# Loads of q, k and v over 128 partitions instead of two halves of 64, and attention matmuls as quarter-array tiles

## The chip, the cores and the metric

The kernel runs on one core of a Trainium2 chip. The metric is device time in microseconds (us), the median of several executions. A ratio is the mean time of one kernel's fast runs over the mean of the other's fast runs of the same rounds on the same chip, with a 95% interval, so it is not quite the ratio of the medians that stand beside it. A profiled execution gives a span, from its first to its last instruction; the run's time is about 2 us longer.

## The reference, cut to what matters

```python
# q, k, v: [8 batches, 8 heads, 576, 64], float32
q_s = softmax(q, over the 64)            # within a row
k_s = softmax(k, over the 576)           # along the sequence
kv  = einsum('bhsd,bhse->bhde', k_s, v)  # 64 x 64 for each head
x   = einsum('bhsd,bhde->bhse', q_s, kv) # then [8, 576, 512], heads side by side
xn  = layer_norm(x) * g_ln
out = x + relu(xn @ w_ch1) @ w_ch2       # 512 -> 2048 -> 512
```

The MLP is most of the work; it runs over nine chunks of 512 tokens (one for each batch, the last for the 64 tokens that each batch has left over). Attention needs 28 MB of q, k and v, in 48 half loads of 590 KB (one tensor, one batch, four of the eight heads).

## The kernel before

The program is written as a list of tasks. A small scheduler puts them in order when the program is built, so that each engine's instructions stand in the program in a fixed order. The scheduler takes the loads' queue to move 0.34 MB per us:

```python
if mb or land:
    queue = max(queue, end) + mb / 0.34
    end = queue + land
```

A half load is two DMAs, each into 64 partitions. Heads 0 to 3 lie on the lower half, heads 4 to 7 on the upper (`R` = `D` = 64, `JT` = 9):

```python
for e in range(2):
    load(stg[s][R * e : R * e + R].rearrange("p (h r) -> p h r", h=2),
         src[b].rearrange("(e h) (p j) d -> e p h (j d)", e=2, j=JT)[e, :, 2 * hf : 2 * hf + 2],
         [("stg", s, e)], 128, 0.295)
```

The queue's DMAs stand in program order too. From batch 2 on, the loads of v stand behind a DMA transpose of exp(q) of the same batch, through `gate`:

```python
lq = [load_half(b, q, hf) for hf in range(2)]
lk = [load_half(b, k, hf) for hf in range(2)]
# ... exp(q), its row sums; for b >= 2:
    state["eqT"] = (plan.add("SP", 0.7, lambda: nc.sync.dma_start_transpose(eqT[u], ...)),)
    gate[0] = state["eqT"]            # loads from here on follow this transpose
lv = [load_half(b, v, hf) for hf in range(2)]
```

TensorE (PE) multiplies exp(k) by v (the kv matmuls) for two heads of one half at a time (weights 64x128, 130 columns), so that half of the result is of no use; VectorE (DVE) scales it and multiplies by a mask, which leaves a block-diagonal weight. That multiplies the transposed exp(q) with the whole array:

```python
for j in range(JT):
    for e in range(2):
        nc.tensor.matmul(pa[ab[e]][:, :130], ek[u][r0 : r0 + R, hf, j, :], vb[u][r0 : r0 + R, hf, j]..., ...)
# DVE: kve[u][:, g, :] = pa * rz * mask
for g in (0, 2, 1, 3):
    nc.tensor.matmul(pa[a], kve[u][:, g, :], et[:, g % 2, 0:8, c0 : c0 + R], ...)
```

ScalarE (ACT) copies the product out as x transposed; a second kind of DMA transpose (`x<-xsT`) brings it back for DVE's batch norm and for the residual. It goes through the same queue as the loads (SPq on the page).

The softmax here doesn't subtract the row's maximum and nothing guards it: scores larger than these inputs give would overflow.

Of the kernel before, what the change touches and what calls it, by code (L numbers as in the profile page):

```python
# [13 lines left out]
FP16 = mybir.dt.float16  # L14
# [119 lines left out]
def dve_t(n, mode=1):  # L134
    return 0.15 + n / (960.0 * mode)
# [3 lines left out]
def kernel(  # L139
# [10 lines left out]
    nc = tc.nc  # L150
# [18 lines left out]
    def sb(shape, dt, name):  # L169
        return persist.tile(shape, dt, name=name, tag=name)  # L170
# [5 lines left out]
    mask = sb([P, P], FP16, "mask")  # L176
# [8 lines left out]
    kve = [sb([P, G, P], FP16, f"kve{i}") for i in range(2)]  # L185
# [27 lines left out]
    def nxt(what, n):  # L213
        i = cnt[what] % n
        cnt[what] += 1
        return i


    def init():
        plan.add("ACT", 1.3, lambda: nc.scalar.add_instruction(mybir.InstLoadActFuncSet(  # L220
            name=nc.get_next_instruction_name(), engine=mybir.EngineType.Activation, act_func_set_id=6)), cls=-1)
        plan.add("DVE", 0.3, lambda: nc.vector.memset(zero.bitcast(U32), 0), w=["zero"])  # L222
        plan.add("DVE", 0.1, lambda: nc.vector.memset(eps, 1e-6 * GS * GS), w=["eps"])
        plan.add("DVE", 0.1, lambda: nc.vector.memset(ones, 1.0 / DM), w=["ones"])
        plan.add("POOL", 1.5, lambda: make_identity(nc, ident), w=["ident"])
        plan.add("POOL", 0.2, lambda: nc.gpsimd.memset(mask.bitcast(U32), 0), w=["mask"])
        for i in range(2):
            plan.add("POOL", 0.1, lambda i=i: nc.gpsimd.memset(mask[64 * i : 64 * i + 64, 64 * i : 64 * i + 64], 1.0), w=["mask"])
        for i in range(2):
            plan.add("POOL", 0.2, lambda i=i: nc.gpsimd.memset(vb[i][:, :, :, :, D], 1.0), w=[("vb", i, h) for h in range(2)])  # L230
        for ko in range(KO1):
            plan.add("ACT", 0.4, lambda ko=ko: nc.scalar.dma_start(
                g_sb[:, ko : ko + 1], moe_g_ln[ko * P : (ko + 1) * P, None]), w=[("g", ko)], land=3.0)
        plan.add("POOL", 0.1, lambda: nc.gpsimd.tensor_scalar_mul(g_sb, in0=g_sb, scalar1=GS),
                 r=[("g", ko) for ko in range(KO1)], w=[("g", ko) for ko in range(KO1)])
# [11 lines left out]
    def load_half(b, src, hf):  # L247

        s = nxt("stg", NST)
        for e in range(2):  # L250
            load(stg[s][R * e : R * e + R].rearrange("p (h r) -> p h r", h=2),
                 src[b].rearrange("(e h) (p j) d -> e p h (j d)", e=2, j=JT)[e, :, 2 * hf : 2 * hf + 2],
                 [("stg", s, e)], 128, 0.295)
        return s
# [24 lines left out]
    def centre_w1(blk):  # L279
# [5 lines left out]
        if blk:  # L285
            plan.add("DVE", dve_t(1024, 2), lambda: nc.vector.tensor_tensor(
                ws, w1_sb[:, 0:2, cs], w1_sb[:, 2:4, cs], op=ALU.add), r=wk, w=["ws"], cls=0)
            src = [ws[:, 0], ws[:, 1]]
        def f():
# [6 lines left out]
            r=["nm"], w=wk, cls=1 if blk == 0 else 0)  # L296
# [16 lines left out]
    def attn(b, early, between=None):  # L313
# [49 lines left out]
        for hf in range(2):  # L363
# [11 lines left out]
            def fm(hf=hf, ab=ab):  # L375
                for j in range(JT):
                    for e in range(2):
                        r0 = R * e
                        nc.tensor.matmul(pa[ab[e]][:, :130], ek[u][r0 : r0 + R, hf, j, :],  # L379
                                         vb[u][r0 : r0 + R, hf, j].rearrange("p s d -> p (s d)"),  # L380
                                         start=(j == 0), stop=(j == JT - 1))
            plan.add("PE", 0.95, fm, r=[("ek", u, hf), ("vb", u, hf)], w=[("pa", a) for a in ab], cls=0)
            for e in range(2):
                a, g = ab[e], 2 * e + hf
                plan.add("DVE", 0.08, lambda a=a, g=g: nc.vector.reciprocal(rz[:, g : g + 1], pa[a][:, D : D + 1]),
                         r=[("pa", a)], w=[("rz", g)], cls=0)
                def fs(a=a, g=g):
                    nc.vector.scalar_tensor_tensor(
                        kve[u][:, g, :].rearrange("p (s d) -> p s d", s=2),
                        in0=pa[a][:, :130].rearrange("p (s c) -> p s c", s=2)[:, :, :D], scalar=rz[:, g : g + 1],  # L390
                        in1=mask.rearrange("p (s d) -> p s d", s=2), op0=ALU.mult, op1=ALU.mult)
                plan.add("DVE", dve_t(128), fs, r=[("pa", a), ("rz", g), "mask"], w=[("kve", u, g)], cls=0)
# [3 lines left out]
        for g in (0, 2, 1, 3):  # L396
            a = nxt("pa", 4)
            c0 = R * (g // 2)
            plan.add("PE", 0.22, lambda g=g, a=a, c0=c0: nc.tensor.matmul(  # L399
                pa[a], kve[u][:, g, :], et[:, g % 2, 0:8, c0 : c0 + R], start=True, stop=True),  # L400
                r=[("eqT", u, g % 2), ("kve", u, g)], w=[("pa", a)], cls=0)
            pv = pa[a].rearrange("p (j t) -> p j t", j=J)
            if early:
                for hf in range(2):
                    js = slice(2 * hf, 2 * hf + 2)
                    w = [("xsT", u, 2 * hf, g), ("xsT", u, 2 * hf + 1, g)]
                    if g // 2 == 0:
                        plan.add("ACT", act_t(256), lambda g=g, js=js, pv=pv: nc.scalar.copy(xt[:, g, js], pv[:, js]), r=[("pa", a)], w=w, cls=0)
                    else:
                        plan.add("DVE", dve_t(256), lambda g=g, js=js, pv=pv: nc.vector.tensor_copy(xt[:, g, js], pv[:, js]), r=[("pa", a)], w=w, cls=0)  # L410
            else:
                plan.add("ACT", act_t(512), lambda g=g, pv=pv: nc.scalar.copy(xt[:, g], pv), r=[("pa", a)],  # L412
                         w=[("xsT", u, j, g) for j in range(J)], cls=0)
        a = nxt("pa", 4)
        def f8(a=a):
            for g in range(G):
                c0 = R * (g // 2)
                nc.tensor.matmul(pa[a][:, R * g : R * g + R], kve[u][:, g, :], et[:, g % 2, 8, c0 : c0 + R], start=True, stop=True)  # L418
        plan.add("PE", 0.3, f8, r=[("eqT", u, 2)] + [("kve", u, g) for g in range(G)], w=[("pa", a)], cls=0)
        c0 = R * (b % 2)  # L420
        plan.add("ACT", act_t(256), lambda a=a: nc.scalar.copy(
            xT8[:, 4 * (b // 2) : 4 * (b // 2) + 4, c0 : c0 + R], pa[a][:, : R * G].rearrange("p (g t) -> p g t", g=G)),
            r=[("pa", a)], w=[("xT8", b)])
# [4 lines left out]
    def tokens(c, cls=1):  # L428

        x, xk, sti, stk = xof(c)  # L430
        if c < B:
            src, r = xsT[c % 2], XK(c % 2)
        else:
            src, r = xT8, [("xT8", b) for b in range(B)]
# [23 lines left out]
    def mm1(c, by_half, split):  # L458

        xt = (xsT[c % 2] if c < B else xT8).rearrange("p (j k) t -> p k j t", j=J)  # L460
        xkeys = XK(c % 2) if c < B else [("xT8", b) for b in range(B)]
# [239 lines left out]
```

## Time and profile before

| | before |
|---|---|
| time, median of 3 executions | 313.81 us (313.08 to 314.52) |
| the profiled execution: its time, its span | 311.52, 309.6 us |
| q, k, v alone in the queue | 230 to 237 GB/s |
| first MLP matmul | 27.07 us |
| first block of 48 wide matmuls of the second chunk | 72.25 us |

The table of waits (engine, what it waited to do, what ended the wait: us in total, times, longest):

```profile
ACT eq L324 <- DMA stg<-in_q_dram: 21.3, 11, 5.2
...
ACT ek L364 <- DMA stg<-in_k_dram: 13.7, 12, 2.5
...
ACT vb L372 <- DMA stg<-in_v_dram: 8.0, 6, 4.1
...
DVE bst L439 <- DMA x<-xsT: 5.4, 4, 2.2
```

Then the page's busy line, and of its DMA issues the transposes of x (last column: median us from issue to landing):

```profile
PE 280.9 (91%) x2017; PEld 173.5 (56%) x2017; DVE 197.4 (64%) x407; ACT 161.8 (52%) x258; POOL 36.6 (12%) x32
```

```profile
x<-xsT SPq DMA_TRANSPOSE x8, 6.4
```

### The profile page before, as it was taken

What the parts mean: (1) busy time and instruction counts of PE and PEld (TensorE: products, weight loads), DVE (VectorE), ACT (ScalarE), POOL (GpSimd) and SP (SyncE); (2) the same over time, 40 slices, a digit from 0 to 9 for tenths busy, and PEclk for the clock granted to TensorE, in tenths of its full rate; (3) what the DMA queues carried; (4) which work ended last, traced back from release to release, by engine and by line L of the source; (5) the groups of instructions that cost most, each with busy time, mean ns of one, the idle gap of its engine ahead of it and who ended that gap; (6) DMA issues with size and microseconds to landing.
All of it is one profiled execution on the core that took longest, in us unless ns stands there. A gap on an engine that the chain in (4) does not pass through costs nothing. (4 is left out here: it accounts for less than half of the span.)

```text
span 309.6 us, 5175 instructions
## 1 busy us (share of the span) xinstructions
PE 280.9 (91%) x2017; PEld 173.5 (56%) x2017; DVE 197.4 (64%) x407; ACT 161.8 (52%) x258; POOL 36.6 (12%) x32
## 2 busy tenths in 40 slices
PE   8749798779999959999898979999999999999992
PEld 3326343445576427845683468447745864784681
DVE  0839999799696516953956499239644973652452
ACT  3625654458774559267556960776388037206500
POOL 2004023005022000050040030201300000000000
PEclk9997999999999979999999999999999999999998
DMA  7999999999996999269989990999993440013004
GB/s 160 267 273 386 280 332 238 236 255 214 228 226 108 196 259 217 54 159 228 233 160 234 286 181 4 210 215 224 160 269 82 83 115 22 2 23 115 0 1 138
DMA packets 56697, 54.74 MB, mean 177 GB/s; under 512 B 35680, under 2 KB 35680, under 8 KB 56672
## 3 DMA queue, kind: packets, MB, share of 16 engines
q1 hardware_dynamic: 56096, 54.41, 75.6%
q8 instruction: 16, 0.26, 0.4%
q10 hardware_dynamic: 576, 0.00, 0.1%
q14 instruction: 9, 0.07, 0.1%
HBM read 36.70 MB, written 9.44 MB: 149 GB/s over the span
## 5 line engine op out<-in xcount | busy, mean ns | idle before, releaser
L450 ACT ACTIVATE hT<-pg 128x512 f16<-128x512 f32 x138 | 80.7, 598 | 61.5 <-PE pg L486 55.3
L486 PE MATMUL pg<-xsT,w_sb 128*128 128x512 f16 x480 | 109.3, 382 | 2.3 <-DVE ot L570 1.2
L486 PEld LDWEIGHTS <-w_sb 128*128 128x128 f16 x544 | 52.7, 98 | 64.8 <-issue 4.4
L502 DVE TENSOR_TENSOR S<-hT 128x1024 f16<-128x1024 f16 x32 | 23.8, 748 | 55.6 <-ACT hT L450 55.6
L562 PEld LDWEIGHTS <-S 128*128 128x128 f16 x512 | 50.0, 98 | 8.0 <-issue 1.4
L562 PE MATMUL pg<-T,S 128*128 128x256 f16 x384 | 43.7, 273 | 1.2 <-DVE cp L570 1.2
L332 POOL TENSOR_TENSOR eq<-eq,rzq 128x1152 bf16<-128x1152 bf16 x12 | 25.8, 2155 | 145.8 <-issue 52.3
L562 PEld LDWEIGHTS <-hT 128*128 128x128 f16 x384 | 37.3, 98 | 7.4 <-issue 1.2
L562 PE MATMUL pg<-w_sb,hT 128*128 128x256 f16 x256 | 30.2, 273 | 0.8 <-ACT hT L450 0.8
L324 ACT ACTIVATE eq<-stg 128x1152 bf16<-128x1152 f32 x16 | 18.6, 1169 | 21.3 <-DMA stg<-in_q_dram 21.3
L439 DVE BATCH_NORM_STATS2 bst<-x 128x6 f32<-128x512 f16 x36 | 24.0, 668 | 5.4 <-DMA x<-xsT 5.4
L327 DVE TENSOR_REDUCE zq<-eq 128x18 f32<-128x1152 bf16 x16 | 21.4, 1340 | 7.3 <-ACT eq L324 7.3
L364 ACT ACTIVATE ek<-stg 128x1152 bf16<-128x1152 f32 x16 | 18.7, 1167 | 13.8 <-DMA stg<-in_k_dram 13.7
L570 DVE SCALAR_TENSOR_TENSOR ot<-pg,st,cp 128x256 f32<-128x256 f32 x48 | 20.9, 477 | 6.9 <-PE pg L562 6.6
L570 DVE SCALAR_TENSOR_TENSOR cp<-pg,st,x 128x256 f32<-128x256 f32 x48 | 20.9, 477 | 4.5 <-PE pg L562 4.3
L379 PE MATMUL pa<-vb,ek 64*128 64x130 f16 x288 | 11.4, 220 | 10.6 <-DVE vb L369 6.6
L372 ACT CAST vb<-stg 128x1152 f16<-128x1152 f32 x12 | 14.0, 1168 | 8.1 <-DMA stg<-in_v_dram 8.0
L379 PEld LDWEIGHTS <-ek 64*128 64x128 bf16 x288 | 9.0, 95 | 15.7 <-issue 12.6
L630 PE MATMUL pg<-zero 128*128 128x512 f16 x51 | 14.8, 447 | 1.2 <-DVE zero L222 1.2
L562 PE MATMUL pg<-T,hT 128*128 128x256 f16 x128 | 15.3, 273 | 0.0
L562 PE MATMUL pg<-w_sb,S 128*128 128x256 f16 x128 | 15.3, 272 | 0.0
L611 PE MATMUL pg<-w_sb,hT 128*128 128x512 f16 x64 | 14.6, 379 | 0.0
(63 smaller groups left out, 215.7 us busy)
## 6 DMA issues: line engine op xcount, KB each, us to landing
stg<-in_q_dram SPq DMA_DIRECT2D x32, 288.0 KB, 7.1
stg<-in_k_dram SPq DMA_DIRECT2D x32, 288.0 KB, 9.6
stg<-in_v_dram SPq DMA_DIRECT2D x32, 288.0 KB, 5.3
out_dram<-ot SPq DMA_DIRECT2D x36, 256.0 KB, 3.7
stg<-in_moe_w_ch_dram SPq DMA_DIRECT2D x16, 512.0 KB, 10.3
x<-xsT SPq DMA_TRANSPOSE x8, 6.4
eqT<-eq SPq DMA_TRANSPOSE x6, 4.6
g_sb<-in_moe_g_ln_dram ACTq DMA_DIRECT2D x4, 0.5 KB, 4.4
```

The source lines that it names most:

```text
L324: plan.add("ACT", act_t(QW), lambda hf=hf, e=e: nc.scalar.activation(e.rearrange("p j (s d) -> p s j d", s=2), sv(lq[hf]), AF.Exp), r=sk(l ...
L327: plan.add("DVE", dve_t(QW), lambda hf=hf, eh=eh: nc.vector.reduce_sum(zq[:, hf], eh, axis=AX.X), r=[("eq", u, hf)], w=[("zq", hf)], cls=cls)
L332: plan.add(eng, dve_t(QW) if early else 2.6, lambda hf=hf, eh=eh, e2=e2: e2.tensor_tensor(eh, eh, rzq[:, hf].to_broadcast([P, 2 * JT, D]), ...
L364: plan.add("ACT", act_t(QW), lambda hf=hf: nc.scalar.activation(ek[u][:, hf].rearrange("p j (s d) -> p s j d", s=2), sv(lk[hf]), AF.Exp), ...
L379: nc.tensor.matmul(pa[ab[e]][:, :130], ek[u][r0 : r0 + R, hf, j, :], vb[u][r0 : r0 + R, hf, j].rearrange("p s d -> p (s d)"), start=(j == ...
L439: plan.add("DVE", dve_t(512), lambda j=j: nc.vector.bn_stats(bst[:, j, :], x[:, j, :]), r=[(xk, j)], w=[("bst", j)], cls=cls)
L450: nc.scalar.activation(hT[:, m, :], pg[gi], AF.Relu)
L486: nc.tensor.matmul(pg[gi], w1_sb[:, ko, m * P : m * P + P], xt[:, ko], start=(ko == 0), stop=(ko == KO1 - 1))
L502: plan.add("DVE", dve_t(256 * n, 2), lambda: nc.vector.tensor_tensor(S[i][:, ks], a, b, op=op), r=r, w=sk(i))
L562: nc.tensor.matmul(pg[gi][:, 256 * i : 256 * i + 256], fa(k, i), fb(k), start=(first and i == 0 and k == 0), stop=(last and k == HK - 1), ...
L570: nc.vector.scalar_tensor_tensor(dst[:, i, :], in0=pg[gi][:, 256 * i : 256 * i + 256], scalar=sti[:, 4, 2 * t0 + i : 2 * t0 + i + 1], in1= ...
L630: nc.tensor.matmul(bank_, zero[:, :P], zero, start=start, stop=start, skip_group_check=True)
```

## The change

The intent is twofold. One DMA for each half load now reaches all 128 partitions, with even heads on the lower half and odd ones on the upper. And the attention matmuls become four concurrent 64x64 tiles, so that no result is thrown away and the mask goes. The core of the diff (cut: buffers, the mask's set-up, the copies of the last 64 tokens, and a few constants of the scheduler):

```diff
-        for e in range(2):
-            load(stg[s][R * e : R * e + R].rearrange("p (h r) -> p h r", h=2),
-                 src[b].rearrange("(e h) (p j) d -> e p h (j d)", e=2, j=JT)[e, :, 2 * hf : 2 * hf + 2],
-                 [("stg", s, e)], 128, 0.295)
+        load(stg[s].rearrange("p (h r) -> p h r", h=2),
+             src[b].rearrange("(h e) (p j) d -> (e p) h (j d)", e=2, j=JT)[:, 2 * hf : 2 * hf + 2],
+             sk(s), 256, 0.59)
...
                     for e in range(2):
-                        r0 = R * e
-                        nc.tensor.matmul(pa[ab[e]][:, :130], ek[u][r0 : r0 + R, hf, j, :],
-                                         vb[u][r0 : r0 + R, hf, j].rearrange("p s d -> p (s d)"), ...)
+                        for i in range(2):
+                            r0, c0 = R * e, D * i
+                            nc.tensor.matmul(pa[ab[e]][c0 : c0 + D, :VW], ek[u][r0 : r0 + R, hf, j, c0 : c0 + D],
+                                             vb[u][r0 : r0 + R, hf, j, i, :], ...)
...
-                    nc.vector.scalar_tensor_tensor(..., in1=mask..., op0=ALU.mult, op1=ALU.mult)
+                nc.vector.tensor_scalar_mul(kve[u][:, g, :], in0=pa[a][:, :D], scalar1=rz[:, g : g + 1])
...
-        for g in (0, 2, 1, 3):
-            nc.tensor.matmul(pa[a], kve[u][:, g, :], et[:, g % 2, 0:8, c0 : c0 + R], ...)
+                for i in range(2):
+                    for e in range(2):
+                        r0, c0 = D * i, R * e
+                        nc.tensor.matmul(pa[ab[i]][c0 : c0 + D, :], kve[u][r0 : r0 + D, 2 * hf + e, :],
+                                         et[r0 : r0 + D, hf, 0:8, c0 : c0 + R], ...)
```

More of the change, by code (lines that the diff above doesn't have):

```diff
@@ L175 @@
     ident = sb([P, P], FP16, "ident")
-    mask = sb([P, P], FP16, "mask")
     zero = sb([P, 512], FP16, "zero")
@@ L184 @@
     eqT = [sb([P, 2 * JT, P], BF16, f"eqT{i}") for i in range(2)]
-    kve = [sb([P, G, P], FP16, f"kve{i}") for i in range(2)]
+    kve = [sb([P, G, D], FP16, f"kve{i}") for i in range(2)]
     xb = [sb([P, J, DM], FP16, f"x{i}") for i in range(3)]
@@ L225, in init @@
         plan.add("POOL", 1.5, lambda: make_identity(nc, ident), w=["ident"])
-        plan.add("POOL", 0.2, lambda: nc.gpsimd.memset(mask.bitcast(U32), 0), w=["mask"])
-        for i in range(2):
-            plan.add("POOL", 0.1, lambda i=i: nc.gpsimd.memset(mask[64 * i : 64 * i + 64, 64 * i : 64 * i + 64], 1.0), w=["mask"])
         for i in range(2):
@@ L232, in init @@
             plan.add("ACT", 0.4, lambda ko=ko: nc.scalar.dma_start(
-                g_sb[:, ko : ko + 1], moe_g_ln[ko * P : (ko + 1) * P, None]), w=[("g", ko)], land=3.0)
-        plan.add("POOL", 0.1, lambda: nc.gpsimd.tensor_scalar_mul(g_sb, in0=g_sb, scalar1=GS),
+                g_sb[:, ko : ko + 1], moe_g_ln[ko * P : (ko + 1) * P, None]), w=[("g", ko)])
+        plan.add("POOL", 4.5, lambda: nc.gpsimd.tensor_scalar_mul(g_sb, in0=g_sb, scalar1=GS),
                  r=[("g", ko) for ko in range(KO1)], w=[("g", ko) for ko in range(KO1)])
@@ L286, in centre_w1 @@
             plan.add("DVE", dve_t(1024, 2), lambda: nc.vector.tensor_tensor(
-                ws, w1_sb[:, 0:2, cs], w1_sb[:, 2:4, cs], op=ALU.add), r=wk, w=["ws"], cls=0)
+                ws, w1_sb[:, 0:2, cs], w1_sb[:, 2:4, cs], op=ALU.add), r=wk, w=["ws"])
             src = [ws[:, 0], ws[:, 1]]
@@ L295, in centre_w1 @@
             w1_sb[:, :, cs], w1_sb[:, :, cs], nm.unsqueeze(1).to_broadcast([P, KO1, 512]), op=ALU.subtract),
-            r=["nm"], w=wk, cls=1 if blk == 0 else 0)
+            r=["nm"], w=wk, cls=0)
     def load_w2(k0, eng="DVE"):
@@ L377, in fm @@
                     for e in range(2):
-                        r0 = R * e
-                        nc.tensor.matmul(pa[ab[e]][:, :130], ek[u][r0 : r0 + R, hf, j, :],
-                                         vb[u][r0 : r0 + R, hf, j].rearrange("p s d -> p (s d)"),
-                                         start=(j == 0), stop=(j == JT - 1))
-            plan.add("PE", 0.95, fm, r=[("ek", u, hf), ("vb", u, hf)], w=[("pa", a) for a in ab], cls=0)
+                        for i in range(2):
+                            r0, c0 = R * e, D * i
+                            nc.tensor.matmul(pa[ab[e]][c0 : c0 + D, :VW], ek[u][r0 : r0 + R, hf, j, c0 : c0 + D],
+                                             vb[u][r0 : r0 + R, hf, j, i, :], start=(j == 0), stop=(j == JT - 1))
@@ L383, in attn @@
+            plan.add("PE", 0.6, fm, r=[("ek", u, hf), ("vb", u, hf)], w=[("pa", a) for a in ab], cls=0)
             for e in range(2):
-                a, g = ab[e], 2 * e + hf
+                a, g = ab[e], 2 * hf + e
                 plan.add("DVE", 0.08, lambda a=a, g=g: nc.vector.reciprocal(rz[:, g : g + 1], pa[a][:, D : D + 1]),
                          r=[("pa", a)], w=[("rz", g)], cls=0)
-                def fs(a=a, g=g):
-                    nc.vector.scalar_tensor_tensor(
-                        kve[u][:, g, :].rearrange("p (s d) -> p s d", s=2),
-                        in0=pa[a][:, :130].rearrange("p (s c) -> p s c", s=2)[:, :, :D], scalar=rz[:, g : g + 1],
-                        in1=mask.rearrange("p (s d) -> p s d", s=2), op0=ALU.mult, op1=ALU.mult)
@@ L392, in attn @@
-                plan.add("DVE", dve_t(128), fs, r=[("pa", a), ("rz", g), "mask"], w=[("kve", u, g)], cls=0)
+                plan.add("DVE", dve_t(64), lambda a=a, g=g: nc.vector.tensor_scalar_mul(
+                    kve[u][:, g, :], in0=pa[a][:, :D], scalar1=rz[:, g : g + 1]),
+                    r=[("pa", a), ("rz", g)], w=[("kve", u, g)], cls=0)
         et = eqT[u].rearrange("p (q j) t -> p q j t", q=2)
         xt = xsT[u].rearrange("p (j k) t -> p k j t", j=J)
-        for g in (0, 2, 1, 3):
-            a = nxt("pa", 4)
-            c0 = R * (g // 2)
-            plan.add("PE", 0.22, lambda g=g, a=a, c0=c0: nc.tensor.matmul(
-                pa[a], kve[u][:, g, :], et[:, g % 2, 0:8, c0 : c0 + R], start=True, stop=True),
-                r=[("eqT", u, g % 2), ("kve", u, g)], w=[("pa", a)], cls=0)
-            pv = pa[a].rearrange("p (j t) -> p j t", j=J)
-            if early:
-                for hf in range(2):
-                    js = slice(2 * hf, 2 * hf + 2)
-                    w = [("xsT", u, 2 * hf, g), ("xsT", u, 2 * hf + 1, g)]
-                    if g // 2 == 0:
-                        plan.add("ACT", act_t(256), lambda g=g, js=js, pv=pv: nc.scalar.copy(xt[:, g, js], pv[:, js]), r=[("pa", a)], w=w, cls=0)
-                    else:
-                        plan.add("DVE", dve_t(256), lambda g=g, js=js, pv=pv: nc.vector.tensor_copy(xt[:, g, js], pv[:, js]), r=[("pa", a)], w=w, cls=0)
-            else:
-                plan.add("ACT", act_t(512), lambda g=g, pv=pv: nc.scalar.copy(xt[:, g], pv), r=[("pa", a)],
-                         w=[("xsT", u, j, g) for j in range(J)], cls=0)
@@ L414, in attn, with fx @@
-        a = nxt("pa", 4)
-        def f8(a=a):
-            for g in range(G):
-                c0 = R * (g // 2)
-                nc.tensor.matmul(pa[a][:, R * g : R * g + R], kve[u][:, g, :], et[:, g % 2, 8, c0 : c0 + R], start=True, stop=True)
-        plan.add("PE", 0.3, f8, r=[("eqT", u, 2)] + [("kve", u, g) for g in range(G)], w=[("pa", a)], cls=0)
-        c0 = R * (b % 2)
-        plan.add("ACT", act_t(256), lambda a=a: nc.scalar.copy(
-            xT8[:, 4 * (b // 2) : 4 * (b // 2) + 4, c0 : c0 + R], pa[a][:, : R * G].rearrange("p (g t) -> p g t", g=G)),
-            r=[("pa", a)], w=[("xT8", b)])
+        for hf in range(2):
+            ab = [nxt("pa", 4) for _ in range(2)]
+            def fx(hf=hf, ab=ab):
+                for i in range(2):
+                    for e in range(2):
+                        r0, c0 = D * i, R * e
+                        nc.tensor.matmul(pa[ab[i]][c0 : c0 + D, :], kve[u][r0 : r0 + D, 2 * hf + e, :],
+                                         et[r0 : r0 + D, hf, 0:8, c0 : c0 + R], start=True, stop=True)
+            plan.add("PE", 0.35, fx, r=[("eqT", u, hf), ("kve", u, 2 * hf), ("kve", u, 2 * hf + 1)], w=[("pa", a) for a in ab], cls=0)
+            for i in range(2):
+                a, g = ab[i], 2 * hf + i
+                pv = pa[a].rearrange("p (j t) -> p j t", j=J)
+                if early:
+                    for th in range(2):
+                        js = slice(2 * th, 2 * th + 2)
+                        w = [("xsT", u, 2 * th, g), ("xsT", u, 2 * th + 1, g)]
+                        if i == 0:
+                            plan.add("ACT", act_t(256), lambda g=g, js=js, pv=pv: nc.scalar.copy(xt[:, g, js], pv[:, js]), r=[("pa", a)], w=w, cls=th / 2)
+                        else:
+                            plan.add("DVE", dve_t(256), lambda g=g, js=js, pv=pv: nc.vector.tensor_copy(xt[:, g, js], pv[:, js]), r=[("pa", a)], w=w, cls=th / 2)
+                else:
+                    plan.add("ACT", act_t(512), lambda g=g, pv=pv: nc.scalar.copy(xt[:, g], pv), r=[("pa", a)],
+                             w=[("xsT", u, j, g) for j in range(J)], cls=0)
@@ new lines, in attn, with f8 @@
+        ab = [nxt("pa", 4) for _ in range(2)]
+        def f8(ab=ab):
+            for hf in range(2):
+                for i in range(2):
+                    for e in range(2):
+                        r0, c0 = D * i, R * e
+                        nc.tensor.matmul(pa[ab[i]][c0 : c0 + D, R * hf : R * hf + R], kve[u][r0 : r0 + D, 2 * hf + e, :],
+                                         et[r0 : r0 + D, hf, 8, c0 : c0 + R], start=True, stop=True)
+        plan.add("PE", 0.2, f8, r=[("eqT", u, 2)] + [("kve", u, g) for g in range(G)], w=[("pa", a) for a in ab], cls=0)
@@ L425, in xof @@
+        c0 = R * (b % 2)
+        for i in range(2):
+            plan.add("ACT", act_t(128), lambda i=i, a=ab[i]: nc.scalar.copy(
+                xT8.rearrange("p (t q s) c -> p t s q c", q=2, s=2)[:, b // 2, i, :, c0 : c0 + R],
+                pa[a][:, : 2 * R].rearrange("p (q t) -> p q t", q=2)),
+                r=[("pa", ab[i])], w=[("xT8", b, i)])
     def xof(c):
@@ L433, in tokens @@
         else:
-            src, r = xT8, [("xT8", b) for b in range(B)]
+            src, r = xT8, [("xT8", b, i) for b in range(B) for i in range(2)]
         i = plan.add("SP", 0.7, lambda: nc.sync.dma_start_transpose(x, src.rearrange("p n t -> p (n t)")) if False else
@@ L460, in mm1 @@
         xt = (xsT[c % 2] if c < B else xT8).rearrange("p (j k) t -> p k j t", j=J)
-        xkeys = XK(c % 2) if c < B else [("xT8", b) for b in range(B)]
+        xkeys = XK(c % 2) if c < B else [("xT8", b, i) for b in range(B) for i in range(2)]
         order = [m + 8 * i for m in range(HK) for i in range(2)] if split else list(range(KO2))
```

## The prediction

> **What bounds the kernel now.** I read the page's busy table first: PE is busy for 280.9 of 309.6 us (91%), DVE for 197.4, ACT for 161.8. Then the chain that ended last: from 225 us to the end it is PE matmuls alone, back to back. So in the later stages a microsecond counts only if it leaves PE's own stream or one of its pauses. Then PE's timeline, for the pauses. Here are the first mm1 matmul, the waits of the second batch's attention, and the longest pause:
>
> ```profile
> 27.07 3.22 PE L473 MATMUL pg<-xsT,w_sb 128*128 128x256 f16 x28
> ...
> 54.56 0.61 PE L341 MATMUL pa<-ident_b,eq 128*128 128x128 bf16 x8 [1.25 <-DVE eq L332]
> ...
> 60.04 0.70 PE L379 MATMUL pa<-vb,ek 64*128 64x130 f16 x18 [1.73 <-DVE vb L369]
> 60.68 1.04 PE L611 MATMUL pg<-w_sb,hT 128*128 128x512 f16 x4
> 62.56 0.70 PE L379 MATMUL pa<-vb,ek 64*128 64x130 f16 x18 [0.85 <-DVE vb L369]
> ...
> 68.08 3.54 PE L473 MATMUL pg<-xsT,w_sb 128*128 128x256 f16 x31 [0.90 <-ACT xsT L408]
> ...
> 111.47 0.72 PE L379 MATMUL pa<-vb,ek 64*128 64x130 f16 x18 [3.32 <-ACT vb L372]
> 112.13 1.89 PE L486 MATMUL pg<-xsT,w_sb 128*128 128x512 f16 x4
> ```
>
> The columns are start, us, then the idle time before and its releaser. Real work of the MLP begins only at 27.07 us (the zero matmuls before it are filler), that of the second chunk at 68.08. Every large pause ends on a cast of v, which itself waited for the load of v (the table of waits has 21.3 us of ACT waiting for q, 13.7 for k, 8.0 for v, and 5.7 of DVE waiting for v). The four matmuls at 112.13 took 1.89 us where such four take about 1.04 elsewhere: the granted clock was 0.50 from 112.0 to 115.4.
>
> Last, windows in which the queue carries one kind of load only: weights over 128 partitions (first and last), and q, k, v in two halves of 64 partitions (the others).
>
> ```profile
> core 0: us, PE busy (x) PEld busy (x) DVE busy (x) ACT busy (x) POOL busy (x), PEclk, DMA share, GB/s
> ...
> 13.60:15.60 2.00, 1.94 (x17) 1.26 (x18) 0.86 (x2) 1.67 (x4) 0.00 (x0) 1.00 1.05 384
> 16.00:20.00 4.00, 2.22 (x10) 0.73 (x8) 0.76 (x2) 1.41 (x3) 0.00 (x0) 1.00 1.06 230
> 22.00:29.00 7.00, 6.03 (x48) 3.43 (x48) 6.51 (x18) 3.00 (x7) 2.02 (x2) 0.76 1.05 387
> 46.00:62.00 16.00, 12.73 (x86) 6.35 (x85) 13.60 (x21) 7.17 (x9) 2.61 (x2) 1.00 1.06 237
> ```
>
> The last two columns are what matter: the DMA engines are fully busy in all four, yet move 385 GB/s into 128 partitions and 230 to 237 into 64. Packets are of like size (2304 and 2048 bytes); in the trace those of the 64-partition loads take about 170 ns, those of the weights 88.
>
> [...] around a group of row-tiled kv matmuls (L379, at 230.6 us) the first starts 96 ns after the stream of the matmul before it should have ended (216 ns after its start), and the next full-array matmul starts 93 ns after the last row-tiled one's 57 ns. [...] The trace has no 64-column load; it hides a 128-column one every 29 ns in the four f8 matmuls (L418).
>
> **The change, part by part.**
>
> *Loads.* Each half of q, k or v is 590 KB. At 231 GB/s it takes 2.55 us, at 385 it takes 1.53: 1.02 us less for each of 48 halves. Where is that on the path?
>
> Stage A, to the first mm1 (27.07 us). Before v's second half come six halves and two weight blocks of 524 KB, 4.59 MB. In the old trace v's last cast starts at 22.16 us. Adding up the trace's packets, each load was usable when about 365 KB more than all bytes up to it had been started. With the same lag, 139 KB in the third microsecond as before and 385 GB/s from 3 us on, v's last half is usable at 3 + (4.59 + 0.365 - 0.14) / 0.385 = 15.5 us, 6.6 us earlier. But DVE then has its queue in the way. By the new program order: its second normalising multiply ends at 12.3 us (first exp at 5.1, then two times 1.35 + 0.27 + 1.36); then two weight scalings, an eqT copy and v's first cast to 14.8; the centring subtraction (L294, 1.22) waits for its matmuls and ends at about 17.1; then two reciprocal/scale pairs (0.9), v's second cast (0.75), copies and weight scalings (1.2), two more pairs (0.9), and the copies and the weight scaling ahead of mm1 (0.9). That gives mm1 at about 21.9 us instead of 27.1: **-5.2 us**.
>
> Stage B, to 44.5 us: PE was busy 15.6 and DVE 16.7 of 17.4 us, so I expect it to keep its length: **0**.
>
> Stage C, to 68.08 us: PE idled 1.25 + 1.73 + 0.85 + 0.90 and a few tenths, together about 5.2 of 23.6 us. DVE was busy 20.7. With q and k of batch 1 landing before 43 us DVE's queue decides: some T sums (5 us), two halves of softmax (6.0), then casts, copies, output scalings and kve, as before. Followed by hand this ends stage C in 19 us: **-4.6 us**.
>
> Stage D, at 111.5 us: v's load is issued behind a store and a DMA transpose that PE's own progress sets (issue at 104.74), so only the transfer shrinks. Usable at about 107.9 and cast by 109.1 instead of 111.4, it cuts the pause from 3.3 to about 1, which I expect to be too short for the half-clock interval (the pauses of 1.7 us and less around 60 us had none; this one cost 3.4 x 0.5 = 1.7 us): **-4 us**. Other pauses of D (5 us together) come from DVE and ACT at the PE's pace: unchanged.
>
> *Matmuls.* The groups concerned before:
>
> ```profile
> L379 PE MATMUL pa<-vb,ek 64*128 64x130 f16 x288 | 11.4, 220 | 10.6 <-DVE vb L369 6.6 <-ACT vb L372 3.8
> L399 PE MATMUL pa<-eqT,kve 128*128 128x512 bf16 x32 | 11.7, 431 | 0.3 <-DVE kve L388 0.2
> L418 PE MATMUL pa<-eqT,kve 128*128 128x64 bf16 x32 | 2.4, 199 | 1.0 <-ACT xsT L412 0.5 <-ACT xsT L408 0.5
> L388 DVE SCALAR_TENSOR_TENSOR kve<-pa,rz,mask 128x128 f16<-128x128 f32 x32 | 11.2, 351 | 1.1
> ```
>
> PE's busy sums overlap, so I count starts. kv: a pair of row tiles every 57 ns, nine pairs, plus two switches of 95: 0.73 us a group. After: nine quads. A quad's stream of 65 columns would be 30 ns[...]. The product with eqT: 2 x 216 ns a group before, no switch; after, four tiles at once, 216 plus two switches of 95 = 406: **nearly 0**. f8: 4 x 29 = 117 ns before, about 60 + 190 after: +0.13 a batch. Some neighbouring groups merge in the new order and save a switch. All eight batches: **about +0.5 us**, against the halving that the array's use suggests (kv and the eqT product hold PE for 18 us).
>
> *DVE and ACT.* The scale of kve loses its mask and half its elements: 351 ns at 128 columns, and about 1 ns a column from the 477 at 256 of the other such operation, so 285 each, 2.1 us of DVE in all, hardly on the path. ACT gets eight more small copies, 1.3 us in all at 52% busy: 0.
>
> Sum: -5.2 - 4.6 - 4 + 0.5 = -13.3. As the three gains stand on hand-followed queues, I take a bit off: -12.8, or **301 us**.
>
> **Rivals.** *Tiles win as meant:* a quad at 30 ns would save 0.24 x 16 = 4 us; with cheap switches 3 to 4 more: 294. For it: row tiles start 3 ns apart. Against: the measured switches[...]. [...] *DVE takes the place of the loads:* it had 96% in B and 88% in C; if the earlier loads only queue before it, A and C give 5 instead of 10: 306. *Wider loads are no faster*, because of q's layout or issue: 313. Against: rows of 2304 contiguous bytes, two a partition, as with the weights.
>
> **Range and chances.** The load gain in A is the surest (4 to 6), C 2 to 5, the pause in D 2 to 5, tiles -5 to +7. Range 295 to 308. Faster by over 2% means under 307.5: 0.87; within 2%: 0.11; slower: 0.02.
>
> **What would show it.** Windows with q, k, v alone at about 385 GB/s; first mm1 near 22 us and the second chunk's near 58; no half-clock interval near 110; kv quads about 57 ns apart, gaps of about 95 ns on both sides of every attention group; the product with eqT at about 0.4 us a group. Wrong would be: mm1's start above 25 us, quads above 80 ns or near 30, or new PE pauses on DVE.

The sum came to -13.3 us, taken as -12.8, or 301 us. Terms are cut from what stands behind it, where they rested on a time for one weight load that no trace or run here shows: the kv term of the tiles, which stood at 0 (quads taken to go by every 57 ns, like the pairs before), so that the sum is the same without it, and a rival in which the tiles' weight loads follow each other (308 to 322 us, the +7 in the range of the tiles). A switch is the 93 to 96 ns that the trace shows on either side of a group of row tiles.

## The result, and the profile after

After: **294.01 us** (293.25 to 294.46, 4 executions), before 313.44 (311.35 to 314.52, 4 executions), ratio 0.9385 (0.9331 to 0.9439). The profiled executions took 293.95 and 311.52, with spans of 291.8 and 309.6. The direction was right, but the gain was larger than the range allowed.

PE's timeline after, at the places that the prediction shows of before (start, us; last the idle time before and its releaser):

```profile
21.51 3.46 PE L475 MATMUL pg<-xsT,w_sb 128*128 128x256 f16 x28
...
48.63 0.61 PE L336 MATMUL pa<-ident_b,eq 128*128 128x128 bf16 x8 [1.13 <-DVE eq L327]
...
52.32 0.48 PE L375 MATMUL pa<-vb,ek 64*64 64x65 f16 x36
...
54.88 0.48 PE L375 MATMUL pa<-vb,ek 64*64 64x65 f16 x36 [0.25 <-DVE vb L364]
...
58.81 3.23 PE L475 MATMUL pg<-xsT,w_sb 128*128 128x256 f16 x28
61.88 10.52 PE L488 MATMUL pg<-xsT,w_sb 128*128 128x512 f16 x48
...
98.06 0.48 PE L375 MATMUL pa<-vb,ek 64*64 64x65 f16 x36 [0.75 <-ACT vb L367]
98.47 1.04 PE L488 MATMUL pg<-xsT,w_sb 128*128 128x512 f16 x4
...
101.58 0.48 PE L375 MATMUL pa<-vb,ek 64*64 64x65 f16 x36 [0.68 <-ACT vb L367]
```

The pauses of 1.73 and 0.85 us in the second batch's attention are 0 and 0.25 us now, and the one of 3.32 is 0.75 and, before the group's second half, 0.68. The four wide matmuls that follow take 1.04 us: there is no interval at half clock before the last microseconds (granted clock 1.00 from 4.5 to 287.8 us, 0.50 in the last 4.0).

Windows with q, k and v alone in the queue (but for some 3% of the second one's packets; last two columns: share of the DMA engines busy, GB/s):

```profile
12.50:15.00 2.50, 2.31 (x19) 1.33 (x19) 1.78 (x5) 1.75 (x4) 0.00 (x0) 1.00 1.06 392
38.60:45.00 6.40, 6.40 (x32) 2.85 (x30) 5.95 (x11) 4.90 (x8) 3.97 (x4) 1.00 1.05 396
```

The groups concerned (busy us, mean ns; then PE's idle time before them):

```profile
L382 DVE TENSOR_SCALAR kve<-pa,rz 128x64 f16<-128x64 f32 x32 | 9.1, 284 | 1.1
L394 PE MATMUL pa<-eqT,kve 64*64 64x512 bf16 x64 | 8.5, 398 | 0.3
...
L375 PE MATMUL pa<-vb,ek 64*64 64x65 f16 x576 | 7.4, 194 | 3.5 <-ACT vb L367 3.0 <-DVE vb L364 0.5
...
L417 PE MATMUL pa<-eqT,kve 64*64 64x64 bf16 x64 | 2.5, 198 | 0.0
```

Twice as many kv matmuls hold PE for 7.4 us instead of 11.4, and the waits before them fell from 10.6 to 3.5 us. The same three views as for the kernel before, waits, busy line and the transposes of x:

```profile
ACT vb L367 <- DMA stg<-in_v_dram: 5.9, 6, 1.5
...
ACT eq L319 <- DMA stg<-in_q_dram: 4.7, 3, 3.5
...
PE pa L375 <- ACT vb L367: 3.0, 5, 0.7
...
ACT ek L359 <- DMA stg<-in_k_dram: 0.8, 2, 0.4
```

```profile
PE 274.1 (94%) x2371; PEld 169.7 (58%) x2371; DVE 192.8 (66%) x407; ACT 161.6 (55%) x266; POOL 35.5 (12%) x29
```

```profile
x<-xsT SPq DMA_TRANSPOSE x8, 4.5
```

ACT's waits for q fell from 21.3 to 4.7 us and for k from 13.7 to 0.8. DVE's wait for x is not in the table any more.

Where the time went, stage by stage. A ends at the first MLP matmul, B at the first one of the second layer (44.51 and 38.71 us), C at the second chunk's first block of 48 wide matmuls (a little later than in the prediction, at a place that every variant has; what that shifts is said below), D at the end of the span:

| stage | before, us | after, us | change | predicted |
|---|---|---|---|---|
| A | 27.07 | 21.51 | -5.56 | -5.2 |
| B | 17.44 | 17.20 | -0.24 | 0 |
| C | 27.74 | 23.17 | -4.57 | -4.6 |
| D | 237.35 | 229.92 | -7.43 | -4, of the tiles' +0.5 most |
| span | 309.6 | 291.8 | -17.8 | -13.3, taken as -12.8 |

D holds the miss. I split D by the starts of PE's matmuls in the trace: what lies between a matmul's own stream (columns / 2.4 + 2.5 ns, a fit to the undisturbed ones of the two traces, whose median steps are 216 ns for 512 columns, 109 for 256 and 55 to 56 for 128) and the next start counts as idle. Before, D has 5.1 us of pauses over 0.3 us at the attention groups and 4.8 us of idle time at all other matmuls; after, 3.3 and 2.4. The attention groups without their pauses fell from 16.3 to 12.8 us. The old half-clock interval (0.50 from 112.0 to 115.4 us) is in these figures, with about 0.6 us in the attention groups and 1.0 at the other matmuls.

The table's C is not quite the prediction's. To the prediction's own boundary, the start of the second chunk's last 28 to 31 matmuls of 256 columns (68.08 us before, 58.81 after), C lost 3.5 us and not 4.6, and D 8.6 and not 7.4.

### The profile page after: what moved, and what is told of

Read it like the earlier page. It is cut to its first block, busy times and chain, and to the rows that moved or that the text cites. A ratio compares the mean times of both kernels' runs of the same rounds, so it can differ in the third digit from the quotient of the medians.

```text
span 291.8 us, 5800 instructions
## 1 busy us (share of the span) xinstructions
PE 274.1 (94%) x2371; PEld 169.7 (58%) x2371; DVE 192.8 (66%) x407; ACT 161.6 (55%) x266; POOL 35.5 (12%) x29
## 4 chain that ended last, share of the span: by engine, by line
PE 66%; DVE 12%; DMA 7%; SPq 7%; ACT 4%; issue 2%; DVEq 0%; ACTq 0%
PE pg L564 32%; PE pg L488 27%; DMA stg<-in_v_dram 6%; SPq L350 5%; PE pg L475 2%; SPq L531 2%; DVE eq L327 2%; DVE zq L322 2%; DMA stg<-in_q_dram 2%; PE pa L394 1%; DVE T L519 1%; PE pa L375 1%; ACT vb L367 1%; DVE ot L572 1%; DVE ot L623 1%
## 5 line engine op out<-in xcount | busy, mean ns | idle before, releaser
L488 PE MATMUL pg<-xsT,w_sb 128*128 128x512 f16 x480 | 107.3, 379 | 0.2 <-DVE w_sb L289 0.2
L488 PEld LDWEIGHTS <-w_sb 128*128 128x128 f16 x544 | 52.1, 98 | 61.2 <-DVE w_sb L289 1.0
L504 DVE TENSOR_TENSOR S<-hT 128x1024 f16<-128x1024 f16 x32 | 21.8, 690 | 52.8 <-ACT hT L452 52.8
L564 PEld LDWEIGHTS <-S 128*128 128x128 f16 x512 | 49.3, 98 | 7.1 <-issue 1.4
L564 PE MATMUL pg<-T,S 128*128 128x256 f16 x384 | 44.3, 273 | 0.0
L322 DVE TENSOR_REDUCE zq<-eq 128x18 f32<-128x1152 bf16 x16 | 21.4, 1335 | 5.5 <-ACT eq L319 5.5
L367 ACT CAST vb<-stg 128x1152 f16<-128x1152 f32 x12 | 13.7, 1166 | 5.9 <-DMA stg<-in_v_dram 5.9
L564 PE MATMUL pg<-w_sb,S 128*128 128x256 f16 x128 | 15.3, 273 | 0.0
L564 PE MATMUL pg<-T,hT 128*128 128x256 f16 x128 | 15.3, 273 | 0.0
L632 PE MATMUL pg<-zero 128*128 128x512 f16 x53 | 14.1, 416 | 1.2 <-DVE zero L221 1.2
L409 ACT CAST xsT<-pa 128x512 f16<-128x512 f32 x24 | 12.8, 587 | 3.5 <-PE pa L394 3.5
L488 PE MATMUL pg<-xT,w_sb 128*128 128x512 f16 x64 | 14.0, 379 | 0.0
```

The costliest lines, as they stand in the source:

```text
L322: plan.add("DVE", dve_t(QW), lambda hf=hf, eh=eh: nc.vector.reduce_sum(zq[:, hf], eh, axis=AX.X), r=[("eq", u, hf)], w=[("zq", hf)], cls=cls)
L367: plan.add("ACT", act_t(QW), lambda vd=vd, va=va: nc.scalar.copy(vd, va), r=sk(lv[hf]), w=[("vb", u, hf)], cls=cls)
L488: nc.tensor.matmul(pg[gi], w1_sb[:, ko, m * P : m * P + P], xt[:, ko], start=(ko == 0), stop=(ko == KO1 - 1))
L504: plan.add("DVE", dve_t(256 * n, 2), lambda: nc.vector.tensor_tensor(S[i][:, ks], a, b, op=op), r=r, w=sk(i))
L564: nc.tensor.matmul(pg[gi][:, 256 * i : 256 * i + 256], fa(k, i), fb(k), start=(first and i == 0 and k == 0), stop=(last and k == HK - 1), ...
```

## The experiments

Two theories were open after this. Either the tiles give what they save on PE (3 us or so) and the loads the rest, or the loads give all of it. Within D: which loads matter, and through which wait?

One experiment that I wanted could not be built: the kernel before with its loads widened and nothing else; no run shows it. So the loads are taken out of the kernel after instead, and the tiles out of both.

**e2: the change with the loads back in halves.** Same head order and same tiles; each load is two DMAs of 64 partitions, at the same place in every engine's order.

```diff
-        load(stg[s]..., src[b].rearrange("(h e) (p j) d -> (e p) h (j d)", ...)[:, 2 * hf : 2 * hf + 2], sk(s), 256, 0.59)
+        def two():
+            for e in range(2):
+                nc.sync.dma_start(stg[s][R * e : R * e + R]..., src[b].rearrange("(h e) (p j) d -> e p h (j d)", ...)[e, :, 2 * hf : 2 * hf + 2])
+        load_by(two, sk(s), 256, 0.59)
```

> The changed kernel with each load of q, k, v issued again as two DMAs of 64 partitions, in the same order on every engine; the quarter tiles stay. Theory (the loads gave about 15 us of the 19.4, the tiles the rest, which the prediction put at zero): 309 us, between 306 and 311, windows of q, k, v alone back at about 235 GB/s, first mm1 back near 27 us, kv groups still 0.51 us of PE. Rival 1 (the tiles give nothing, as predicted, and the loads gave it all): 313 us.

Measured: 313.59 us, ratio 1.0039 (1.0010 to 1.0067), as the theory that the tiles give nothing had it. The tiles and all the rest of the change, without the wide loads, give nothing. Windows with loads alone are back at 231 GB/s, PE waits for v and DVE waits for x:

```profile
16.00:20.00 4.00, 2.64 (x13) 0.90 (x10) 1.52 (x3) 2.19 (x4) 0.00 (x0) 1.00 1.06 231
```

```profile
DVE bst L447 <- DMA x<-xsT: 8.3, 5, 2.6
...
PE pa L381 <- ACT vb L373: 6.6, 7, 1.5
...
PE pa L381 <- DVE vb L370: 5.4, 4, 3.0
```

**e3: as many DMAs as e2, but all over 128 partitions.** Each half load is split by head, two DMAs of 295 KB.

```diff
+            for h in range(2):
+                nc.sync.dma_start(stg[s][:, h * 576 : h * 576 + 576], src[b]...[:, 2 * hf + h])
```

> The changed kernel with each load again as two DMAs of 295 KB, but each over all 128 partitions (one head of each pair of groups). Theory (what counts is how many partitions are reached): 294 us within 1.5, 385 GB/s. Rival 2 (half as many and twice as large DMAs gave the gain): 305 us or more, rate and start of mm1 as with the halves.

Measured: 295.87 us, ratio 0.9487 (0.9465 to 0.9508), so 0.4 us outside the theory's margin and far from the rival; 408 GB/s in a window of loads alone (two fifths of the packets are weights). So it is the partitions reached, not the number or the size of the DMAs (e2, with as many DMAs of the same size, moves 231). In the halves the packets took about 170 ns instead of 93, so the DMA engines looked fully busy in both cases (share 1.05 to 1.06). A half load was two DMAs, one into each half, and no run loads one half alone. The twice as many DMAs cost about 1% beside the change (by the ratios, from different rounds).

**e7 and e8: two tiles at a time.** The order of the kv matmuls is meant to let only two row tiles run together; e7 with wide loads, e8 with halves. The product with exp(q) was cut in 256-column pieces for the same end.

```diff
-                for j in range(JT):
-                    for e in range(2):
-                        for i in range(2):
+                for i in range(2):
+                    for j in range(JT):
+                        for e in range(2):
```

> The changed kernel with the order of the kv matmuls (column tile outermost) and of the product with eqT (in two pieces of 256 columns, column tile or row tile outermost) such that only two tiles can run at a time; the loads stay wide. Theory: kv groups 0.73 us instead of 0.51, eqT groups about 0.6 instead of 0.31 to 0.51, 16 of each, so about 299 us (297 to 301). Rival 1 (the tiles give nothing): 294 to 295 us.

> Both undone: loads in halves of 64 partitions and two tiles at a time. Theory (the two add up and nothing else in the change matters): 312 to 316 us, so the kernel before within 1%. Rival 3 (the change of order in the queues, or the smaller DVE operation, gave part of it): 310 us or less.

Measured: e7 294.48 us, ratio 0.9445 (0.9431 to 0.9459), beside 0.9385 (0.9331 to 0.9439) for the change in other rounds; e8 314.29, ratio 1.0051 (0.9996 to 1.0105). For the kv matmuls the edit worked (busy 10.1 us instead of 7.4, a group 0.66 to 0.67 us instead of 0.48); the product's pieces took 0.42 to 0.49 us a group in D, and 0.41 to 0.49 after the change, one group of 0.66 aside, so that part was not undone. The theory of e7 failed and its rival held; the theory of e8 held. e7's profile:

```profile
L375 PE MATMUL pa<-vb,ek 64*64 64x65 f16 x576 | 10.1, 194 | 2.2 <-ACT vb L367 1.7 <-DVE vb L364 0.3
```

PE's time in D's attention without pauses rose by 1.9 us over the change, its pauses fell by 1.4. Most of what four tiles save, PE spends waiting for v.

**e9 and e10: wide loads only early, only later.** e9 has wide loads for batches 0 and 1 and halves for the others, e10 the reverse. All else is the kernel after.

```diff
+        if b < 2:      # e10: b >= 2
             load(...)  # 128 partitions
+            return s
+        load_by(two, ...)  # two halves
```

> The kernel with the loads in halves, but batches 0 and 1 loaded over 128 partitions. Theory (wide loads are worth 10 us up to the second chunk and 8 us later, and these add): 303 us, between 301.5 and 305; second chunk's mm1 near 58 us, then the stage to the end 231 to 232 us as with the halves. Prediction's view (later loads are worth 4 us at most): 299 us or less.

> The kernel with the loads in halves, but batches 2 to 7 loaded over 128 partitions. Theory: the stage from the second chunk on takes 223 to 225 us instead of 231.75, and DVE's wait of 8.3 us for the transposes of x is gone, so about 305 us (303.5 to 307). Prediction's view: 309 us or more.

Measured: e9 301.38 us, ratio 0.9677 (0.9658 to 0.9697); e10 302.64, ratio 0.9716 (0.9697 to 0.9736). The second chunk's block of 48 starts at 61.61 us in e9 (after: 61.88) and 70.35 in e10. D, from there to the end, is 237.9 us in e9 and 229.95 in e10. So the early loads are enough for the whole gain in A and C, and all of D's gain belongs to the later ones (e10 reaches the block 1.9 us before the kernel before did, for a reason that was not looked for); the two shares (3.2% and 2.8%) add up to about the whole (6.2%). Both times are a little below the ranges of the theory that they add, and clear of the prediction's view. The transposes of x and DVE's wait, e9 and then e10 (where DVE has no such wait):

```profile
x<-xsT SPq DMA_TRANSPOSE x8, 7.4
```

```profile
x<-xsT SPq DMA_TRANSPOSE x8, 4.6
```

**e13 and e14: later v alone, later q and k alone.** D's gain of 7.4 to 8 us against the predicted 4 is still without a cause. e13 is the kernel after with only v of batches 2 to 7 in halves; e14 has only q and k of those in halves.

```diff
-        if b >= 2:
+        if b < 2 or src is not v:      # e14: src is v
             load(...)  # 128 partitions
```

> The kernel after, in which v alone of batches 2 to 7 is loaded in two halves of 64 partitions; everything else is loaded over 128. Theory of the prediction (in stage D only the transfer of v matters, the loads of q and k are hidden): stage D loses what the change gained there, so it grows from 230 to 234-238 us and the time to 298-302. Rival (any slow load holds the queue and the engines that wait in program order behind it; v is a third of the loads): stage D 231-233, time 295-297.

> The other way round: q and k of batches 2 to 7 in halves of 64 partitions, v and batches 0 and 1 over 128. Theory of the prediction: q and k are loaded long before they are needed, stage D stays at 230 us, time 294-295. Rival (the loads of q and k hold the queue, so that transposes and ScalarE's casts behind them come late): stage D 233-237, time 297-301, with VectorE's wait for x back at 5 us or more or ScalarE's waits for q and k twice as long as after the change.

Measured: e13 299.12 us, ratio 0.9586 (0.9538 to 0.9634); e14 299.74, ratio 0.9603 (0.9558 to 0.9648). By stages:

| later loads in halves | D, us | pauses at attention | idle at the other matmuls |
|---|---|---|---|
| none (after) | 229.9 | 3.3 | 2.4 |
| v (e13) | 234.3 | 7.8 | 2.4 |
| q and k (e14) | 236.1 | 7.0 | 4.3 |
| q, k and v (e9) | 237.9 | 7.9 | 6.0 |

Slow loads of v alone cost 4.4 us: this is about the predicted 4, and it lies wholly in pauses at the attention groups. But slow loads of q and k alone, which the prediction took to be hidden, cost 6.2. About 1.7 of these are an interval at half clock (the four wide matmuls below take 1.89 us, where such four take 1.04), which neither e13 nor e9 has in D before its last microseconds (every such four of theirs takes 1.04); it follows a pause of 1.96 us:

```profile
163.49 0.72 PE L386 MATMUL pa<-vb,ek 64*64 64x65 f16 x36 [1.96 <-ACT vb L378]
164.13 1.89 PE L499 MATMUL pg<-xsT,w_sb 128*128 128x512 f16 x4
```

The two overlap, to 8.0 for all. Each line of the table is one execution, that of e13 the fastest of its four; the ratios of e13 and e14 do not differ beyond their intervals, so which of the two costs more is not shown. That q and k cost something on top of v is: e9's ratio lies clear of e13's. The first expectation of e13 and the rival of e14 held. Here is one way in which q and k reach PE: the fourth batch's kv groups on PE's timeline, in e13 and then in e14:

```profile
98.09 0.48 PE L386 MATMUL pa<-vb,ek 64*64 64x65 f16 x36 [1.23 <-ACT vb L378]
...
102.21 0.48 PE L386 MATMUL pa<-vb,ek 64*64 64x65 f16 x36 [1.28 <-ACT vb L378]
```

```profile
97.85 0.48 PE L386 MATMUL pa<-vb,ek 64*64 64x65 f16 x36 [0.77 <-ACT vb L378]
...
102.72 0.48 PE L386 MATMUL pa<-vb,ek 64*64 64x65 f16 x36 [1.91 <-ACT vb L378]
```

In e14 the second half of v is itself a wide load, issued at 94.67 us as in the kernel after (94.86); q and k follow it in the queue at once. It took 6.8 us to land instead of 5.5, and PE's pause for it grew from 0.68 to 1.91. What the queue carries behind a load moved its landing: in the slice of the page in which most of its transfer falls, the DMAs moved 259 GB/s in e14 (from 96.8 to 104.2 us) and 350 after the change (from 94.8 to 102.1). How the engines come to do that is not shown. Other waits of e14:

```profile
ACT eq L330 <- DMA stg<-in_q_dram: 8.1, 5, 3.6
...
ACT ek L370 <- DMA stg<-in_k_dram: 7.2, 9, 1.7
...
DVE bst L452 <- DMA x<-xsT: 3.4, 3, 2.2
```

ACT's wait for q and k together is 15.3 us instead of 5.5 (in D alone 10.0 instead of 0.2), and DVE's wait for x is back in part.

**e12: halves, with the transposes of x ahead of k.** Is DVE's wait for x the second path into D? This is e2 with the later loads of k ordered behind the transposes of x of the batch before.

```diff
         lq = [load_half(b, q, hf) for hf in range(2)]
+        if not early:
+            gate[0] = state["x"]
         lk = [load_half(b, k, hf) for hf in range(2)]
...
-            tokens(b)
+            state["x"] = (tokens(b),)
```

> The kernel after with every load in two halves of 64 partitions (the variant that took 313.6 us), and now the loads of k of the later batches ordered behind the transposes of x of the batch before, so that these no longer queue behind slow loads. Theory (in stage D the slow loads cost time through the transposes of x, which hold VectorE's batch norm and so TensorE): VectorE's wait for x falls from 8.3 us to under 2, the gaps of stage D outside attention fall from 6.1 towards 2.5 us, and the time to 308-310 us, although the loads stay slow. Rival (the wait for x is harmless, or only moves): 313 +- 1 us.

Measured: 310.74 us (308.5 to 311.49, before 313.44), ratio 0.9886 (0.9828 to 0.9944). Between the two expectations, so I look at D. DVE's wait went, as meant, and ACT's wait for k took its place (34.5 us; 14.8 in e2):

```profile
ACT ek L367 <- DMA stg<-in_k_dram: 34.5, 13, 6.3
...
DVE bst L449 <- DMA x<-xsT: 0.2, 1, 0.2
```

D is 237.7 us against 237.3 in e2, its idle time at the other matmuls 5.9 against 6.1. The gain lies ahead of D: the block of 48 begins at 71.96 instead of 74.73 us, where e2's second chunk had run its first 28 matmuls at half clock (4.88 us instead of 3.23). So taking the wait for x away did not shorten D. But D of e12 holds an interval at half clock, from 91.6 us, that e2's does not; it follows a pause of 1.96 us for a cast of v, and 24 matmuls of 256 columns in it take 3.95 us, where such 24 take 2.78 elsewhere in D. It cost about 1.7 us, 1.2 of them at the other matmuls, whose idle time would otherwise be about 4.7. The scheduler also made another order of PE's work. An estimate from these numbers is that the wait for x is worth up to 1.3 us of D: a part of the cause at most. It is one of several places where slow loads surface; mended there, they surface at ACT.

**e5 and e11: v not behind the transpose.** After the change PE still waits 3 us for casts of v. The loads of v may be issued before the transpose of exp(q). e11 is the same with the order of tiles of e7.

```diff
             state["eqT"] = (plan.add("SP", 0.7, ...),)
-            gate[0] = state["eqT"]
```

> The changed kernel, with the loads of v of the later batches no longer ordered behind the DMA transpose of exp(q). Theory (the pauses of PE that are left at kv come from v's load standing behind that transpose): PE's waits for ACT's cast of v, 3.0 us, go to under 0.5, and the time to 291 us (289.5 to 292.5). Rival 4 (v in front only delays the transposes of x and q behind it): 294 to 297 us, with new waits of DVE for x or of PE for the transposed q.

> As the last, with two kv tiles at a time as in the run of pairs. If four tiles at once save 0.2 us a kv group, and this was lost to the wait for v, it shows here: 1.9 to 3 us over e5_v_early. If some other wait takes the saving up again: equal to it within 0.7 us.

Measured: e5 **289.43 us**, ratio 0.9289 (0.9276 to 0.9302); e11 291.92, ratio 0.9366 (0.9353 to 0.9379), in the same five rounds. e5 beats both kernels: its profiled span is 287.3 us against 291.8 after the change (by the ratios, from different rounds, the step is 1.0%). Of PE's waits for casts of v only this one is left in e5's table of waits, none on ACT; below it stands the kv group:

```profile
PE pa L374 <- DVE vb L363: 0.5, 2, 0.3
```

```profile
L374 PE MATMUL pa<-vb,ek 64*64 64x65 f16 x576 | 7.7, 194 | 0.5 <-DVE vb L363 0.5
```

The time of e5 is a shade below its expected range, that of e11 within it. With the wait for v out of the way, four tiles at a time instead of two are worth 2.5 us. Behind that wait they were worth nothing that e7 could show.

**e6: the same edit in the kernel before.**

> The kernel before, in which the loads of v alone may start before the transpose of exp(q) has been issued; nothing else is changed, the loads stay in halves of 64 partitions. Theory (in the kernel before the pause for v in stage D is worth 5 us and an earlier start of the same slow loads removes it): 306-307 us, against 311.5. Rival (the queue is so full of slow loads that what v gains the transposes of x lose): 309-313 us, with VectorE's wait for x above the 5.4 us of before.

Measured: 335.40 us (334.03 to 336.03), ratio 1.0690 (1.0644 to 1.0736). Neither expectation held. The fourth batch's first kv group on PE's timeline:

```profile
101.78 1.16 PE L378 MATMUL pa<-vb,ek 64*128 64x130 f16 x18 [5.76 <-ACT vb L371]
```

The order that the scheduler made now has this group earlier: it ran at 101.78 us, after a pause of 5.76, and at 111.47 in the kernel before. But v now stands in the queue behind q and k of its own batch; it took 10.1 us to land instead of 5.3 (medians), and PE waited for ACT's casts of v for 21.4 us in all. Around such pauses it ran at half clock: five intervals from 98 to 245 us, 23.9 us together, against one of 3.4 in the kernel before (mean granted clock of the profiled runs 0.953 and 0.984). The longer landing alone does not make the loss, as v's went from 5.5 to 9.6 us in e5 too. The scheduler reckons with 0.34 MB per us, and the loads in halves move 0.23: an order built on transfers that the chip doesn't make turns into pauses. In the kernel after, loads alone move 0.39, and the same edit gains time. That the rate in the scheduler is the reason is my reading; I ran no kernel with that constant changed.

## Why the prediction was right or wrong

**Loads, the rate: right.** 385 GB/s was expected, 392 and 396 stand in the windows. e3 (408) beside e2 (231) shows that the partitions decide it.

**Stages A, B and C: right.** -5.2, 0 and -4.6 were predicted; -5.6, -0.2 and -4.6 measured. e9 shows that the early loads are enough for A and C. The queues followed by hand were good to 0.4 us at the first MLP matmul (21.9 against 21.51). To the prediction's own boundary C gave 3.5, a quarter less than foreseen but within its range, and the three stages 9.3 of 9.8.

**Stage D: this step failed.** The prediction had "so only the transfer shrinks" for v, -4 us, and "Other pauses of D (5 us together) come from DVE and ACT at the PE's pace: unchanged". The size of the first half held: v alone is worth 4.4 us (e13), the pause at 111 us went to 0.75 and 0.68, and the half-clock interval with it. Its path did not, so the size was luck in part. At that pause v's first half was to be usable 3.2 us after its issue at 104.74; it took 4.75 us after the change and 5.44 before (both DMAs), so the transfer gave 0.7 us. The other 1.8 came because v was issued 5.2 us before PE ran out of work, and not 3.4. In the kernel before, DVE waited for x ahead of the output that the store in front of v carries (DVE, then the queue):

```profile
97.25 0.69 DVE L439 BATCH_NORM_STATS2 bst<-x 128x6 f32<-128x512 f16 x1 [2.21 <-DMA x<-xsT]
97.86 0.86 DVE L570 SCALAR_TENSOR_TENSOR ot<-pg,st,cp 128x256 f32<-128x256 f32 x2
```

```profile
98.75 1.32 SPq L529 DMA_DIRECT2D out_dram<-ot  x2
100.17 4.51 SPq L355 DMA_TRANSPOSE eqT<-eq  x1
104.74 1.31 SPq L241 DMA_DIRECT2D stg<-in_v_dram  x2
```

After the change x landed there in 4.4 us instead of 6.8, and the output also stands ahead of the batch norm in DVE's order; no run separates these two. The second half was wrong. The other pauses came in good part from loads of q and k that looked hidden because PE never waits for them by name. In the traces ACT waits for them, which casts v and writes the hidden layer in a fixed order; the transposes of x, which stand in the same queue, land later; and so does a wide load of v with slow ones behind it. Slow q and k cost 6.2 us alone, a half-clock interval included, and 3.6 on top of slow v (237.9 less 234.3; by the medians of the times 2.3). That is the term missing from the sum. Its size depends on the tiles: with two kv tiles at a time, as before the change, all wide loads together give D 5.7 us (236.35 in e8, 230.65 in e7), with four 7.4 (e2 and after). I first took DVE's wait for x to be the way it came; e12 took that wait away and D stayed, though with a half-clock interval that may hide a part. How the 3.6 us divide between ACT, the transposes and the landing of v stays open.

**The base: 2.3 us too high.** The gains were read in a profile whose execution took 311.52 us and taken off the median of 313.81. From 311.52 the same sum gives 298.7, and the measured stages, 17.8 us, lead to 293.7 against 293.95.

**Tiles: about right in time, wrong about the quads.** (A slip in the sum: nine pairs at 57 ns and two switches of 95 make 0.70 us; the 0.73 that the trace has comes from pairs 60 ns apart.) The prediction had "kv quads about 57 ns apart". Line L375 at 52.32 us shows 36 matmuls of 194 ns in 0.48 us, so nine quads start within 0.29 us, some 35 ns apart (the median step in the trace is 33; the four of the first quad start within 10), which is nearer to the 30 that the prediction names as a sign of being wrong. The product with exp(q) holds PE for 0.33 to 0.51 us a group where nothing else holds it up, and about 0.4 was expected. The gaps of 93 to 97 ns at each side of the kv groups were as predicted (115 behind the two places where two groups merge); behind the product it is 117. A kv group thus holds PE for 0.51 us instead of 0.73, and the rival "Tiles win as meant" was right about PE. But no time came of it: e2 is no faster than before, and e7 not shown slower than the change. Most of the saved time ends in a wait for v. e11 against e5 shows it come back, 2.5 us, once v is early. The allowance of +0.5 us and the half microsecond taken off were thus both to the wrong side.

**DVE and ACT: right.** 285 ns predicted for the scale of kve, 284 measured. One reading of the prediction was too broad: of the pauses that it lists, that of 1.25 us ends on DVE's softmax of q and that of 0.90 on a copy of xsT, not on a cast of v.

Together: 2.3 us from the base, about 3.9 in D (-7.4 against -4 and +0.5), 0.6 in A and B, 0.5 taken off: 7.3 us (to the prediction's own boundary D has 5.1, and C takes 1.1 back). The profiled run of after is 0.2 us longer beyond its span than that of before, so 7.1, the difference between 301 and 293.95.

## What to carry to other kernels

Look at how many partitions each load reaches before looking at anything on TensorE: here the whole of the gain went when that was undone (e2, 313.59 us). When a shared queue gets faster, count all of its users, also those that the bounding engine never waits for by name (slow q and k alone cost D 6.2 us in e14), and test a supposed chain of waits by removing one link, as it may only move. Work saved on an engine that then waits is not lost but waiting for the next change: after the loads of v were moved ahead, the tiles gave their 2.5 us (e11 against e5).
